# Two-operand elementwise work to VectorE, one-operand copies to GpSimd: batch 0 and the w_out conversion of an attention and feed-forward kernel

## The chip, the cores and the metric

The kernel runs on one core of one Trainium2 chip. The metric is device time in microseconds (us) of one execution, lower is better. Three executions of the kernel before took 678.16, 678.62 and 679.0 us; the median, 678.62, is the figure to which the change is compared.

## The reference

Per head (4 batches, 8 heads, 576 tokens, 64 wide), causal softmax attention is mixed with a linear-attention memory by a gate; the result, seen as 2304 tokens of 512, goes through a feed-forward block with squared ReLU.

```python
scores = scale * q @ k.T                       # causal mask, softmax -> a
local  = a @ v
q_p    = where(q > 0, q, exp(q) - 1) + 1
mem    = (q_p @ M_prev) / (q_p @ z_prev + 1e-6)
x      = g * mem + (1 - g) * local             # g = sigmoid(beta), per head
h = x @ w_in                                   # 512 -> 2048
out = (s * relu(h)**2 + b) @ w_out             # 2048 -> 512
```

## The kernel before

Most large matmuls are done in a fast fp32 format as three products: an operand is split into a high part H (a copy that rounds) and a low part L (the operand minus H), and H*H, H*L and L*H are added in PSUM. So each operand costs one copy and one two-operand subtraction on an elementwise engine, and which of VectorE (DVE), ScalarE (ACT) and GpSimd (POOL) does these is what the change is about.

The first phase walks over 16 pairs of heads. The four pairs of batch 0 (`g < NP`, where `NP` is 4) use plain fp32 operands: `s_red` (line 311) reduces scores from PSUM on DVE and writes them to `P`, `s_exp` (L319) exponentiates on ACT, `s_norm` sums (L326, L327 on DVE) and scales `P` (L331; engine chosen by `dve("nm", ...)`), `pt_bank` transposes `P` on TensorE (L370) and ACT copies it back (L353), `av_mm32` multiplies, and `av_evac` copies the result from PSUM (L432). `x_split` splits that into H (L448) and L (L449). `phi_a` to `phi_c` prepare the memory's queries, `split_qk` (L229) splits scores' operands. Beside all this `w_in` is converted: sixteen `split_w` read 64-bit words with `conv64` (L81 to L84), then make H (L467) and L (L468). `mm1` (L479 to L481, the first feed-forward product) of batch 0 is woven between the heads of batch 1 and so on; its ReLU (`mm1_out`, L488) is on ACT and goes to DRAM.

When attention is done, only `mm1` of the last batch is left on TensorE (PE). Under it `w_out` is converted in eight steps: `conv_u` twice (L81 to L84 on tile `stg`), `t_u` (L654 to L657, sums for a Strassen-like product with seven block products), `split_u` (copies L660 and L664, subtractions L665). `late_b` (L671, L673) makes the H and L of two more blocks; its low part writes into the place of `w1H`, so it waits for the end of `mm1`. The second phase (`t` from 0 to 8) makes for each of seven block products `m` and two halves `c` an operand: `operand` forms a sum or difference for some `m` (L714, L716, L718), its H (L719) and L (L720); `product` (L728 to L730) multiplies, `combine` adds up and stores.

Times at which the helpers are called are a hand-written table of positions (`T`, `at(...)`); the framework then orders each engine's instructions by a timing model of its own. An engine executes its list in order, so an instruction that waits holds up all that stand behind it.

```python
def dve(nm, n, i=None):
    t = T[nm][len(JOBS[n][1])]
    return nc.vector if (t if i is None else t[i]) else nc.gpsimd
```

By `T`, in all pairs of five tiles the third tile's scaling L331 (320 columns) is on DVE and the other four on POOL; the second of the two subtractions of `split_qk` is on DVE and the first on POOL; `x_split`'s subtraction is on POOL.

Of the kernel before, what the change touches and what calls it, by code (L numbers as in the profile page):

```python
# [8 lines left out]
F32 = mybir.dt.float32  # L9
# [3 lines left out]
ALU = mybir.AluOpType  # L13
# [17 lines left out]
def attention_moe_kernel(  # L31
# [15 lines left out]
    nc = tc.nc  # L47
# [87 lines left out]
    def dve(nm, n, i=None):  # L135

        t = T[nm][len(JOBS[n][1])]
        return nc.vector if (t if i is None else t[i]) else nc.gpsimd
# [62 lines left out]
    def phi_b(g):  # L201
        p, r, z = st["q", g], st["r", g], st["z", g]
        nc.vector.scalar_tensor_tensor(p, p, 1.0, r, ALU.min, ALU.add)
        nc.gpsimd.tensor_mul(r, p, z.unsqueeze(1).to_broadcast([128, 5, 2, D]))

    def phi_c(g):
        p, r = st["q", g], st["r", g]
        hp = 2 * parts(g)[1]
        n = ap2.tile([128, 5, 2, 1], F32, tag="nrm", name="nrm")
        nc.vector.tensor_reduce(n, r, AX.X, ALU.add)  # L210
        nc.vector.scalar_tensor_tensor(
            n, n, 1e-6, gin[:, hp:hp + 2].unsqueeze(1).unsqueeze(3).to_broadcast([128, 5, 2, 1]), ALU.add, ALU.mult)
        nc.vector.reciprocal(n, n)
        nc.gpsimd.tensor_mul(p, p, n.to_broadcast([128, 5, 2, D]))

# [208 lines left out]
    def av_evac(x, hi, ps):  # L424
# [6 lines left out]
        if x < 2 * NP:  # L431
            nc.vector.tensor_copy(xo[ma, :], ps[0:64, :n])  # L432
            return
# [24 lines left out]
    def split_w(n):  # L458
# [7 lines left out]
        else:  # L466
            nc.gpsimd.tensor_scalar(H, w, 1.0, 1.0, ALU.mult, ALU.mult)  # L467
        (nc.vector if T["wd"][n] else nc.gpsimd).tensor_sub(L, w, H.bitcast(F32))  # L468

# [180 lines left out]
    def t_u(i, w, s):  # L650
# [5 lines left out]
        nc.vector.tensor_sub(t2, b22, t1)  # L656
        nc.gpsimd.tensor_sub(late32[:, i, 0], t2, b21)  # L657

    def split_u(i, w, s):
        pin(nc.scalar.copy(late32[:, i, 1], w[:, 2]))  # L660
        bHs[i] = w2.tile([128, 5, NE], F32R, tag=f"row{i}", name="bH")
        for x, a, n in ((w[:, 0:1], 0, 1), (w[:, 3:4], 1, 1), (s[:, 0:3], 2, 3)):
            L, H = bLs[:, i, a:a + n], bHs[i][:, a:a + n]
            pin(nc.scalar.copy(H, x))  # L664
            nc.vector.tensor_sub(L, x, H.bitcast(F32))  # L665
# [35 lines left out]
    def operand(t, m, c):  # L701
# [9 lines left out]
        if m in (7, 3):  # L711
            y = x
            x = SUM[c]
            nc.gpsimd.tensor_sub(x, y, A[{7: 21, 3: 11}[m]])  # L714
        elif m == 5:
            nc.vector.tensor_add(x, x, A[22])  # L716
        elif m == 6:
            nc.vector.tensor_sub(x, A[21], x)  # L718
        nc.scalar.copy(H, x)  # L719
        (nc.gpsimd if m in ONPOOL else nc.vector).tensor_sub(L, x, H.bitcast(F32))  # L720

# [143 lines left out]
```

## Time and profile before

| | |
|---|---|
| runs, us | 678.16, 678.62, 679.0 (median 678.62) |
| the profiled execution: its time, its span | 676.45, 674.7 |
| mean granted TensorE clock | 0.98 of full speed |
| busy share of the span: PE, DVE, ACT, POOL | 94%, 72%, 69%, 61% |
| first phase with batch 0 | up to about 122 us |
| w_out conversion on DVE begins | 423.81 us |
| last mm1 matmul ends, first product begins | 477.15 us, 476.99 us |

The span is from the first to the last instruction of the profiled execution; its own time is 1.75 us longer and 2.17 us under the median of the runs. A row for a group of instructions gives their count, their busy time in us, the mean of one in ns, and the idle time of their engine just before them with what ended most of it. Busy time of PE includes time in which matmuls run at a lowered clock.

### The profile page before, as it was taken

Reading aid. Unit: us, or ns where it says so; the run is one execution under the profiler, and the core shown is the slowest. Engines: PE = TensorE matmul, PEld = TensorE weight load, DVE = VectorE, ACT = ScalarE, POOL = GpSimd, SP = SyncE. Lnnn points to the kernel's source line nnn. Section 1 sums busy time; section 2 is a strip of 40 time slices with the busy share of each in tenths; the row PEclk is TensorE's granted clock in tenths of the full one; section 3 lists DMA queues with packets and bytes.
Section 4 is the critical chain, followed back from the end, with each engine's and each line's share of the span. In section 5 each row is a group of like instructions: output and inputs, shape, how many; then the busy total and the mean of one; then the engine's idle time right before and its main releaser. Section 6 shows DMA issues by size and latency. Waiting matters only on the chain. (4 is left out here: it accounts for less than half of the span.)

```text
span 674.7 us, 13026 instructions
## 1 busy us (share of the span) xinstructions
PE 634.6 (94%) x4536; PEld 576.8 (85%) x4536; DVE 487.2 (72%) x1090; ACT 464.0 (69%) x1037; POOL 409.3 (61%) x405
## 2 busy tenths in 40 slices
PE   5989898999999999999999999997699999999998
PEld 2545565889998999999998999997699999999998
DVE  4888879878667757766866641798968887568674
ACT  5566675767667767766866753579888878586841
POOL 3799988776555556555645351341387776666583
PEclk9998899999999999999999999997889999999999
DMA  7987778496677678688875623796643543435301
GB/s 267 232 238 177 197 187 215 161 234 166 166 207 202 165 218 214 162 224 193 198 211 133 162 77 97 286 298 206 206 110 118 165 138 98 116 105 157 94 24 40
DMA packets 73442, 115.75 MB, mean 172 GB/s; under 512 B 10016, under 2 KB 51232, under 8 KB 73376
## 3 DMA queue, kind: packets, MB, share of 16 engines
q1 hardware_dynamic: 73376, 114.91, 61.1%
q8 instruction: 36, 0.59, 0.4%
q14 instruction: 30, 0.25, 0.1%
HBM read 57.68 MB, written 23.59 MB: 120 GB/s over the span
## 5 line engine op out<-in xcount | busy, mean ns | idle before, releaser
L319 ACT ACTIVATE P<-P,mn 128x64 f32<-128x64 f32 (+4 forms) x160 | 89.4, 560 | 48.3 <-DVE mn L311 47.6
L730 PE MATMUL yps<-bH,op 128*128 128x256 f32 x360 | 102.7, 287 | 5.5 <-DVE op L720 5.5
L331 POOL TENSOR_SCALAR P<-P,sm,omg 128x64 f32<-128x64 f32 (+3 forms) x128 | 86.0, 684 | 33.4 <-ACT xc L436 13.5
L728 PE MATMUL yps<-bH,op 128*128 128x256 f32 x360 | 102.7, 286 | 1.3 <-ACT op L719 1.3
L729 PE MATMUL yps<-bL,op 128*128 128x256 f32 x360 | 102.8, 285 | 0.0
L311 DVE CUSTOM_DVE_ANT_0 P<-sps,mask 128x64 f32<-128x64 f32 (+4 forms) x160 | 65.6, 423 | 29.9 <-PE sps L298 23.3
L479 PE MATMUL hps<-xs,w1H 128*128 128x320 f32 (+1 forms) x256 | 79.4, 310 | 5.0 <-ACT r L488 4.8
L479 PE MATMUL hps<-xs,w0H 128*128 128x320 f32 (+1 forms) x256 | 78.8, 310 | 1.6 <-ACT r L488 0.8
L370 PE MATMUL tps<-ident,P 128*128 128x128 f32 (+2 forms) x480 | 76.1, 277 | 2.2 <-POOL P L331 1.3
L481 PE MATMUL hps<-xs,w1L 128*128 128x320 f32 (+1 forms) x256 | 76.9, 300 | 0.0
L480 PE MATMUL hps<-xs,w1H 128*128 128x320 f32 (+1 forms) x256 | 76.8, 300 | 0.0
L480 PE MATMUL hps<-xs,w0H 128*128 128x320 f32 (+1 forms) x256 | 76.2, 299 | 0.0
L481 PE MATMUL hps<-xs,w0L 128*128 128x320 f32 (+1 forms) x256 | 76.1, 298 | 0.0
L730 PEld LDWEIGHTS yps<-bH,op 128*128 128x128 f32 x360 | 69.1, 193 | 6.5 <-DVE op L720 6.4
L728 PEld LDWEIGHTS yps<-bH,op 128*128 128x128 f32 x360 | 69.2, 193 | 1.6 <-ACT op L719 1.6
L729 PEld LDWEIGHTS yps<-bL,op 128*128 128x128 f32 x360 | 69.6, 193 | 0.0
L297 PE MATMUL sps<-X 128*128 128x192 f32 (+1 forms) x180 | 59.9, 337 | 6.1 <-DVE mn L311 3.8
L370 PEld LDWEIGHTS tps<-ident,P 128*128 128x128 f32 (+2 forms) x480 | 55.6, 132 | 11.6 <-issue 5.9
L488 ACT ACTIVATE r<-hps 128x320 f32<-128x320 f32 (+1 forms) x128 | 50.1, 408 | 21.4 <-PE hps L481 15.1
L479 PEld LDWEIGHTS hps<-xs,w1H 128*128 128x128 f32 x256 | 49.3, 193 | 6.5 <-ACT r L488 5.5
L298 PE MATMUL sps<-X 128*128 128x192 f32 (+1 forms) x180 | 53.8, 303 | 0.0
L479 PEld LDWEIGHTS hps<-xs,w0H 128*128 128x128 f32 x256 | 48.8, 191 | 3.9 <-ACT r L488 1.8
(131 smaller groups left out, 1944.5 us busy)
## 6 DMA issues: line engine op xcount, KB each, us to landing
X<-sqk SPq DMA_DIRECT2D x60, 432.0 KB, 6.3
r_d<-r SPq DMA_DIRECT2D x32, 320.0 KB, 4.5
qks<-in_qk_t_dram SPq DMA_DIRECT2D x15, 576.0 KB, 6.5
xa<-in_moe_w_in_dram SPq DMA_DIRECT2D x16, 512.0 KB, 6.4
r_d<-r SPq DMA_DIRECT2D x32, 256.0 KB, 4.3
raw<-in_moe_w_out_dram SPq DMA_DIRECT2D x16, 512.0 KB, 6.7
w1L<-r_d SPq DMA_DIRECT2D x16, 512.0 KB, 4.7
Q<-sqp SPq DMA_DIRECT2D x48, 144.0 KB, 4.1
```

What stands on the lines that cost most here:

```text
L297: nc.tensor.matmul(ps[:, :m], lhsT=lhsT, rhs=X[:, 1, c0:c0 + m], start=True, stop=False)
L298: nc.tensor.matmul(ps[:, :m], lhsT=lhsT, rhs=X[:, 2, c0:c0 + m], start=False, stop=True)
L311: nc.vector.tensor_tensor_reduce(P[:, PO[i] + c0:PO[i] + c0 + n], ps[:, :n], mask[:, mo:mo + n], -SCALE, init, ALU.add, ALU.min, mn[:, o:o ...
L319: nc.scalar.activation(pt, pt, AF.Exp, scale=-1.0, bias=mn[:, o:o + 1], accum_out=sm[:, i:i + 1])
L331: dve("nm", x // 2, i).tensor_scalar(pt, pt, sm[:, i:i + 1], omg[:, h:h + 1], ALU.mult, ALU.mult)
L370: nc.tensor.transpose(ps[0:kn, o:o + qn], P[0:qn, c:c + kn], ident[0:qn, 0:qn])
L479: nc.tensor.matmul(ps, lhsT=wH[:, p, fs], rhs=xs[:, 0], start=p == 0, stop=False)
L480: nc.tensor.matmul(ps, lhsT=wH[:, p, fs], rhs=xs[:, 1], start=False, stop=False)
L481: nc.tensor.matmul(ps, lhsT=wL[:, p, fs], rhs=xs[:, 0], start=False, stop=p == NP - 1)
L728: nc.tensor.matmul(ps, lhsT=H, rhs=BH, start=f == 0, stop=False)
L729: nc.tensor.matmul(ps, lhsT=H, rhs=BL, start=False, stop=False)
L730: nc.tensor.matmul(ps, lhsT=L, rhs=BH, start=False, stop=f == KF - 1)
```

## The change

Within batch 0 (`n < NP` or `g < NP`) every subtraction and product of two tiles goes to VectorE and all five scalings L331 to GpSimd; the copy L432 from PSUM goes to ScalarE. The subtraction L468 of all sixteen `split_w` goes to VectorE. In the w_out conversion L657 goes from GpSimd to VectorE and the copies L660 and L664 from ScalarE to GpSimd. For the first 256 tokens of the second phase (`t == 0`) the H copies go from ScalarE to GpSimd and the differences L714 and the low parts L720 of `m` in 1, 2, 4 from GpSimd to VectorE. The numbers of DMAs, of matmuls and of all other instructions stay, and so do the bytes. In the changed file a line has a number greater by 2 (from L137 of before), and from L713 by 2 to 5.

```diff
--- before.py
+++ after.py
@@ -134,6 +134,8 @@
 
     def dve(nm, n, i=None):
 
+        if n < NP:
+            return nc.gpsimd if nm == "nm" else nc.vector
         t = T[nm][len(JOBS[n][1])]
         return nc.vector if (t if i is None else t[i]) else nc.gpsimd
 
@@ -201,7 +203,7 @@
     def phi_b(g):
         p, r, z = st["q", g], st["r", g], st["z", g]
         nc.vector.scalar_tensor_tensor(p, p, 1.0, r, ALU.min, ALU.add)
-        nc.gpsimd.tensor_mul(r, p, z.unsqueeze(1).to_broadcast([128, 5, 2, D]))
+        (nc.vector if g < NP else nc.gpsimd).tensor_mul(r, p, z.unsqueeze(1).to_broadcast([128, 5, 2, D]))
 
     def phi_c(g):
         p, r = st["q", g], st["r", g]
@@ -211,7 +213,7 @@
         nc.vector.scalar_tensor_tensor(
             n, n, 1e-6, gin[:, hp:hp + 2].unsqueeze(1).unsqueeze(3).to_broadcast([128, 5, 2, 1]), ALU.add, ALU.mult)
         nc.vector.reciprocal(n, n)
-        nc.gpsimd.tensor_mul(p, p, n.to_broadcast([128, 5, 2, D]))
+        (nc.vector if g < NP else nc.gpsimd).tensor_mul(p, p, n.to_broadcast([128, 5, 2, D]))
 
 
     def evac(H_out, L_out, ps, key):
@@ -429,7 +431,7 @@
         xo = st["x", g, hi]
         ma = slice(64 * j, 64 * j + 64)
         if x < 2 * NP:
-            nc.vector.tensor_copy(xo[ma, :], ps[0:64, :n])
+            nc.scalar.copy(xo[ma, :], ps[0:64, :n])
             return
         xc = ap1.tile([128, 320], F32, tag="xc", name="xc")
         co = slice(64 - 64 * j, 128 - 64 * j)
@@ -465,7 +467,7 @@
             nc.scalar.copy(H, w)
         else:
             nc.gpsimd.tensor_scalar(H, w, 1.0, 1.0, ALU.mult, ALU.mult)
-        (nc.vector if T["wd"][n] else nc.gpsimd).tensor_sub(L, w, H.bitcast(F32))
+        nc.vector.tensor_sub(L, w, H.bitcast(F32))
 
 
     def mm1(b, c, f, half):
@@ -654,14 +656,14 @@
         nc.vector.tensor_sub(t1, b12, w[:, 0])
         nc.vector.tensor_sub(t3, b22, b12)
         nc.vector.tensor_sub(t2, b22, t1)
-        nc.gpsimd.tensor_sub(late32[:, i, 0], t2, b21)
+        nc.vector.tensor_sub(late32[:, i, 0], t2, b21)
 
     def split_u(i, w, s):
-        pin(nc.scalar.copy(late32[:, i, 1], w[:, 2]))
+        pin(nc.gpsimd.tensor_scalar(late32[:, i, 1], w[:, 2], 1.0, 1.0, ALU.mult, ALU.mult))
         bHs[i] = w2.tile([128, 5, NE], F32R, tag=f"row{i}", name="bH")
         for x, a, n in ((w[:, 0:1], 0, 1), (w[:, 3:4], 1, 1), (s[:, 0:3], 2, 3)):
             L, H = bLs[:, i, a:a + n], bHs[i][:, a:a + n]
-            pin(nc.scalar.copy(H, x))
+            pin(nc.gpsimd.tensor_scalar(H, x, 1.0, 1.0, ALU.mult, ALU.mult))
             nc.vector.tensor_sub(L, x, H.bitcast(F32))
 
     def late_b(n, part):
@@ -711,13 +713,16 @@
         if m in (7, 3):
             y = x
             x = SUM[c]
-            nc.gpsimd.tensor_sub(x, y, A[{7: 21, 3: 11}[m]])
+            (nc.vector if t == 0 else nc.gpsimd).tensor_sub(x, y, A[{7: 21, 3: 11}[m]])
         elif m == 5:
             nc.vector.tensor_add(x, x, A[22])
         elif m == 6:
             nc.vector.tensor_sub(x, A[21], x)
-        nc.scalar.copy(H, x)
-        (nc.gpsimd if m in ONPOOL else nc.vector).tensor_sub(L, x, H.bitcast(F32))
+        if t == 0:
+            nc.gpsimd.tensor_scalar(H, x, 1.0, 1.0, ALU.mult, ALU.mult)
+        else:
+            nc.scalar.copy(H, x)
+        (nc.gpsimd if m in ONPOOL and t else nc.vector).tensor_sub(L, x, H.bitcast(F32))
 
     def product(t, m):
         ps = ps_y.tile([128, NE], F32, tag="y", name="yps")
```

The framework's order of every engine's list follows from the changed instructions too. Three places of it are shown.

VectorE in batch 0, around the copies of one pair's result (before; `x_561` and `x_568` are the two halves of the result of the second pair, L331 the scaling of `P`):

```order
L331 TENSOR_SCALAR P<-P,sm,omg 128x320
L311 ISA P,mn<-sps,mask 128x320
L311 ISA mn 128x1
L432 COPY x_561<-ops 64x256
...
L82 TENSOR_SCALAR w<-w 128x512
L311 ISA P,mn<-sps,mask,mn 128x288
L311 ISA mn 128x1
L83 SCALAR_TENSOR_TENSOR w<-xa,w 128x512
L84 SCALAR_TENSOR_TENSOR w<-xa,w 128x512
L203 SCALAR_TENSOR_TENSOR qs<-qs,phr 128x640
L432 COPY x_568<-ops 64x320
```

The same place in the changed kernel:

```order
L83 SCALAR_TENSOR_TENSOR w<-xa,w 128x512
L470 TENSOR_TENSOR w0L<-w,w0H 128x512
L451 TENSOR_TENSOR xs<-x_561,xs 128x256
L84 SCALAR_TENSOR_TENSOR w<-xa,w 128x512
...
L329 RECIPROCAL sm<-sm 128x5
...
L313 ISA P,mn<-sps,mask 128x192
L313 ISA mn 128x1
L470 TENSOR_TENSOR w0L<-w,w0H 128x512
L82 TENSOR_SCALAR w<-w 128x512
L451 TENSOR_TENSOR xs<-x_568,xs 128x320
```

The copies and the scaling have left VectorE's list; the low parts of `w_in` (L470, L468 of before) and of the result (L451, L449 of before) stand in it instead, and wait for GpSimd's copies.

GpSimd under the last `mm1`, at the start of the w_out conversion, before:

```order
L449 TENSOR_TENSOR xs<-x_5204,xs 128x320
L657 TENSOR_TENSOR late_5399<-stg 128x256 x4
L714 TENSOR_TENSOR sum_5400<-w0L 128x512
L657 TENSOR_TENSOR late_5399<-stg 128x256 x3
L720 TENSOR_TENSOR op<-w0L,op 128x512 x2
```

and in the changed kernel:

```order
L451 TENSOR_TENSOR xs<-x_5204,xs 128x320
L662 TENSOR_SCALAR late_5399<-stg 128x256
L666 TENSOR_SCALAR bH<-stg 128x256 x2
L666 TENSOR_SCALAR bH<-stg 128x768
L662 TENSOR_SCALAR late_5399<-stg 128x256
```

GpSimd's list is four copies per step there (L662 and L666 are L660 and L664 of before), and one subtraction less.

VectorE where `mm1` ends: L673 waits for its last matmul. Before:

```order
L84 SCALAR_TENSOR_TENSOR stg<-raw,stg 128x512
L673 TENSOR_TENSOR w1H<-late_5399,w0H 128x1024
L673 TENSOR_TENSOR w1H<-late_5399,w0H 128x1024 x2
L655 TENSOR_TENSOR stg<-stg 128x256
L656 TENSOR_TENSOR stg<-stg 128x256
L718 TENSOR_TENSOR w0L<-w0L 128x4x128
L720 TENSOR_TENSOR op<-sum_5400,op 128x512
L665 TENSOR_TENSOR bL<-stg,bH 128x256 x2
L665 TENSOR_TENSOR bL<-stg,bH 128x768
```

and in the changed kernel (L675 is L673 of before, L667 L665, L725 the low part L720):

```order
L725 TENSOR_TENSOR op<-w0L,op 128x512
L675 TENSOR_TENSOR w1H<-late_5399,w0H 128x1024
L675 TENSOR_TENSOR w1H<-late_5399,w0H 128x1024 x2
L667 TENSOR_TENSOR bL<-stg,bH 128x768
L83 SCALAR_TENSOR_TENSOR stg<-raw,stg 128x512
L725 TENSOR_TENSOR op<-w0L,op 128x512
L84 SCALAR_TENSOR_TENSOR stg<-raw,stg 128x512
L725 TENSOR_TENSOR op<-sum_5400,op 128x512
L720 TENSOR_TENSOR w0L<-w0L 128x4x128
L84 SCALAR_TENSOR_TENSOR stg<-raw,stg 128x512
```

More of the conversion (one L83, two L84, one wide L665) now stands behind L673, and the two low parts of the first product (L725 from `w0L`), which were GpSimd's, stand around it.

## Rows read from the trace of the kernel before

**Rows 1.** The page's first part: busy time, share and instructions of each engine.

```profile
PE 634.6 (94%) x4536; PEld 576.8 (85%) x4536; DVE 487.2 (72%) x1090; ACT 464.0 (69%) x1037; POOL 409.3 (61%) x405
```

**Rows 2.** Stretches: length; busy us of PE, PEld, DVE, ACT, POOL; PEclk; DMA.

```profile
20.00:122.00 102.00, 91.64 (x441) 57.01 (x442) 85.96 (x214) 65.28 (x169) 91.86 (x98) 0.95 0.83 211
122.00:400.00 278.00, 273.57 (x2033) 259.50 (x2032) 194.47 (x563) 197.41 (x536) 157.86 (x188) 1.00 0.70 182
423.00:476.00 53.00, 47.68 (x339) 46.77 (x338) 47.05 (x92) 41.90 (x84) 17.42 (x9) 0.94 0.73 256
476.00:500.00 24.00, 17.79 (x116) 16.98 (x115) 19.26 (x23) 21.59 (x36) 12.96 (x10) 0.79 0.56 167
500.00:660.00 160.00, 157.66 (x1313) 156.24 (x1313) 118.86 (x149) 119.61 (x173) 112.08 (x79) 1.00 0.38 112
```

**Rows 3.** PE's waits from 20 to 122 us: us in total, times, longest.

```profile
PE sps L297 <- DVE mn L311: 2.8, 5, 1.0
PE ops L402 <- DVE x L432: 2.7, 4, 1.1
PE sps L297 <- DVE sm L327: 2.0, 1, 2.0
```

**Rows 4.** VectorE's groups by line from 20 to 122 us.

```profile
L83 DVE SCALAR_TENSOR_TENSOR w<-xa,w 128x512 uint32<-128x512 uint32 x12 | 12.7, 1061 | 0.1
L84 DVE SCALAR_TENSOR_TENSOR w<-xa,w 128x512 uint32<-128x512 uint32 x12 | 10.0, 830 | 0.1
L432 DVE COPY x<-ops 64x256 f32<-64x256 f32 (+1 forms) x16 | 7.2, 448 | 4.1 <-PE ops L405 4.0
L82 DVE TENSOR_SCALAR w<-w 128x512 uint32<-128x512 uint32 x12 | 7.0, 584 | 1.2 <-ACT w L81 1.2
L326 DVE TENSOR_SCALAR sm<-sm 128x5 f32<-128x5 f32 x9 | 6.3, 698 | 1.1 <-ACT P L319 1.1
L331 DVE TENSOR_SCALAR P<-P,sm,omg 128x320 f32<-128x320 f32 x10 | 5.9, 591 | 0.1
...
L327 DVE RECIPROCAL sm<-sm 128x5 f32<-128x5 f32 x9 | 1.6, 183 | 0.1
```

**Rows 5.** VectorE's groups by line from 423 to 476 us.

```profile
L83 DVE SCALAR_TENSOR_TENSOR stg<-raw,stg 128x512 uint32<-128x512 uint32 x16 | 10.9, 685 | 0.1
...
L82 DVE TENSOR_SCALAR stg<-stg 128x512 uint32<-128x512 uint32 x16 | 6.9, 433 | 10.3 <-ACT stg L81 10.3
...
L656 DVE TENSOR_TENSOR stg<-stg 128x256 f32<-128x256 f32 x7 | 2.9, 417 | 0.0
```

**Rows 6.** PE in order of time: start, us, instruction, idle before it and releaser.

```profile
459.73 0.63 PE L479 MATMUL hps<-xs,w1H 128*128 128x320 f32 x1 [4.40 <-ACT r L488]
...
484.01 0.39 PE L730 MATMUL yps<-bH,op 128*128 128x256 f32 x1 [4.03 <-DVE op L720]
```

**Rows 7.** GpSimd's groups by line from 20 to 122 us.

```profile
L468 POOL TENSOR_TENSOR w0L<-w,w0H 128x512 fp32r<-128x512 f32 x8 | 10.9, 1367 | 0.0
L204 POOL TENSOR_TENSOR phr<-qs,z 128x640 f32<-128x640 f32 x5 | 9.7, 1945 | 1.4 <-DVE qs L203 1.4
L449 POOL TENSOR_TENSOR xs<-x,xs 128x256 fp32r<-128x256 f32 (+1 forms) x8 | 7.8, 980 | 0.0
L214 POOL TENSOR_TENSOR qs<-qs,nrm 128x640 f32<-128x640 f32 x5 | 7.6, 1521 | 0.9 <-PE sps L298 0.9
...
L468 POOL TENSOR_TENSOR w1L<-w,w1H 128x512 fp32r<-128x512 f32 x4 | 5.1, 1274 | 0.1
...
L467 POOL TENSOR_SCALAR w0H<-w 128x512 fp32r<-128x512 f32 x7 | 5.0, 709 | 3.8 <-DVE nrm L211 2.5 <-DVE w L84 1.3
```

**Rows 8.** ScalarE's groups by line from 423 to 476 us.

```profile
L664 ACT CAST bH<-stg 128x256 fp32r<-128x256 f32 (+1 forms) x21 | 10.8, 555 | 2.3 <-DVE stg L656 2.3
```

**Rows 9.** VectorE in order of time, at the end of mm1.

```profile
477.06 4.49 DVE L673 TENSOR_TENSOR w1H<-late,w0H 128x1024 fp32r<-128x1024 f32 x3 [1.51 <-PE hps L480]
```

**Rows 10.** Waits from 420 to 500 us: us in total, times, longest.

```profile
DVE stg L82 <- ACT stg L81: 10.3, 6, 5.8
```

## The prediction

> **What bounds the kernel now.** First the engines' totals: PE is busy for 634.6 us, far ahead of the others [rows 1], so time can be won only where PE stands still or runs at a lowered clock. The stretches say where [rows 2]. From 122 to 400 us PE is busy for 273.6 of 278 us, from 500 to 660 for 157.7 of 160, both at full clock: what the other engines do there costs next to nothing. Two stages are different. In batch 0 (20 to 122 us) PE has 10.4 us of gaps and a mean clock of 0.95, worth 5.1 us more. From 423 to 500 us, under the w_out conversion and at the handover to the second phase, it has 5.3 + 6.2 us of gaps, at clocks of 0.94 and 0.79. The change acts on just these two stages.
>
> The waits name what ends last. In batch 0 the busiest engine is POOL, 91.9 of 102 us [rows 2], yet PE's long waits are for DVE: 2.8 us for minima, 2.7 for copies of results, 2.0 for sums [rows 3]. DVE is busy for 86.0 us, and part of that is not work: L83 takes 1061 ns there [rows 4] and 685 under the w_out conversion, where POOL has little to do [rows 2, 5]; L326, on five columns, takes 698 where its neighbour L327 on the same tile takes 183 [rows 4]. So POOL's load reaches PE by way of DVE's durations. In the second stage PE stands still for 4.40 us because ACT comes late with the ReLU that frees PSUM, and for 4.03 us because DVE comes late with a low part of the second product [rows 6].
>
> **Batch 0, part by part.** *Removed from DVE*: 16 copies L432, 7.2 us, and 8 of the 10 scalings L331 (those of batch 0), 8 x 0.591 = 4.7 us [rows 4]; together 11.9. *Added to DVE*: in this window 12 low parts L468, 8 low parts L449, L204 and L214 for three of the five pairs seen there, and 3 subtractions L229. None of these runs on DVE before in this shape, so I price them by columns from the nearest two-operand row, L83 at 685 ns for 512 columns [rows 5]: 12 x 0.685 + 8 x 0.385 + 6 x 0.856 + 3 x 0.771 = 8.2 + 3.1 + 5.1 + 2.3 = 18.7 us. That is the low end; if all met POOL as L83 does now, it would be 1061/685 as much, 29.0 us. Net +6.8 at the low end, +17.1 at the high.
>
> *Relief.* On the groups of rows 4 alone the time above the free price is 12 x (1061 - 685) + 12 x (830 - 685) + 12 x (584 - 433) + 9 x (698 - 183) ns = 4.5 + 1.7 + 1.8 + 4.6 = 12.6 us [rows 4, 5]. POOL loses 16.0 us of L468, 7.8 of L449 and three fifths of 17.3 of L204 and L214, 34 of the 41 us of two-operand work in rows 7, and gains 8 scalings, some 4.7 us; it falls from 92 to some 62 us. I take away half of the 12.6, 6.3 us: less than POOL's two-operand time falls, since its copies and scalings stay and DVE has 29 more instructions that can meet them. Bounds: 0 and 12.6.
>
> *Waits.* DVE's 4.0 us of waiting in front of L432 [rows 4] goes: ACT waits there instead, which has 36.7 us free in the stretch [rows 2] and behind which stand exponentials and transposed copies. What is new is that DVE waits for POOL's H copies (20 times). The order gives each some DVE instructions of distance, and a copy takes 0.709 us [rows 7]; I put 1 us in all, between 0 and 20 x 0.36 = 7. ScalarE gains 16 copies of about 0.45 us, hidden in those 36.7 us; were they not, they would hold up the exponentials by up to 7 us.
>
> Sum for the stage: +6.8 - 6.3 - 4.0 + 1.0 = **-2.5 us** of DVE's time. I let PE follow DVE one for one, because PE's three waits above are all for DVE.
>
> **The handover.** ACT loses the copies: 10.8 us of L664 by 476 us [rows 8], and L660 and the fourteen H copies of `t == 0` besides. The 4.40 us gap before 459.73 should go, as ACT's list then holds little but ReLUs, L81 and the squaring. But that gap hides: DVE reaches L673 at 475.6 and waits only 1.51 us for the end of mm1 [rows 9], so an earlier end of mm1 gives DVE at most those 1.5 us. Beyond that DVE sets the pace. Ahead of L673 it gains seven L657 at 0.417 (priced as L656, the same shape) [rows 5], one L714 and one L720 at 0.685, 4.3 us; a wide L665, an L83 and two L84, some 3.0 us, move behind. Of its 10.3 us of waiting for L81 the longest, 5.8, lies ahead of the conversion [rows 10]; of the other 4.5 us I take half, 2.2, as saved by the freed ACT. POOL's copies beside it cost DVE some 1 us. So L673 starts 1.5 - 1.3 + 2.2 - 1.0 = 1.4 us earlier. From there to the low part that ended the 4.03 us gap it was 4.49 us of L673 and on to 484.01, 6.9 us in all [rows 6, 9]; now it is three L673, the wide L665, L83, L720, L84, L720, about 7.3. That part comes 1.0 us earlier; the low parts of the eighth step of w_out, which the first product needs, come some 3 us behind it, against PE's 2 us of work, so the small later stalls stay. **-1 us**, between -8 (both gaps and their lowered clock gone) and +6 (PE waits for the whole of DVE's extra 4.3 us, and longer at half clock).
>
> No DMA is added, dropped or resized; w_out's rows are loaded into places that the H copies free, now in POOL's list, which is all but empty there (17.4 of 53 us [rows 2]). SP's queue passes the same transfers.
>
> **The sum.** 676.45 - 2.5 - 1.0 = 672.95 for the profiled execution, which lies 2.17 us under the median of the runs; so I expect **675.1 us** against 678.62.
>
> **The rivals.** *A, slower: DVE becomes the engine that never catches up in batch 0.* It is the only one of the three whose free-price work grows, from 86 us busy of 102. If the 18.7 us cost the middle between free and contended, 23.8, relief is only 4 us, and the waits for POOL's copies are 4 us, then 23.8 - 11.9 - 4 - 4 + 4 = +8, and with the handover 685.6 us. It decides as soon as relief and DVE's saved wait are under 7.9 us together. For it: POOL still has 62 us of work, and it holds up mostly the instructions that DVE now has more of. Against: L83 at 685 ns beside a lightly loaded POOL. The Trainium skill (SBUF — State Buffer, Who interferes with whom) states that a DVE instruction with two SBUF inputs contends with any GpSimd instruction that reads SBUF, and that the later one is blocked to the other's end; by that rule one-operand copies block as well, which is this rival's case, and no row above separates them from the two-operand ones.
>
> *B, no change.* The two stages are set by DVE's total, relief equals the added work less the saved waits, and the 4.40 us gap is given back at L673: 678.6 us. For it: mm1's end was waited for by DVE for just 1.51 us.
>
> *C, much faster.* PE's gaps go: 10 of the 15.5 us in batch 0 (gaps and clock) need only that DVE be in time, and the two gaps in rows 6 take half a clock of several us with them; half of each stage's loss is 8 + 8 us, to 662.6. Against: DVE has more to do, not less.
>
> **How the numbers follow.** My forecast (a gain of 1.4 to 9 us) has 0.42, C 0.13, B 0.15, A 0.24, and a handover that gets worse by more than batch 0 gains 0.06. A measurement of this kernel can tell 0.2%, 1.36 us, from no change. So faster 0.55, same 0.15, slower 0.30. The range runs from 666, half way to C, to 685, just short of A's full price; 2 in 10 lie outside.
>
> **What would show it.** In the changed profile: L83 in batch 0 under 900 ns and L326 under 450; POOL near 62 us from 20 to 122 us; no L432 among PE's waits; no 4 us gap of PE for L488, but still one of 3 to 7 us for a low part after mm1. It is wrong if DVE in batch 0 is busy over 95% with PE waiting for it longer than now (A), or if new rows of DVE waiting for POOL's copies add up to more than 3 us; and wrong the other way if PE's gaps in batch 0 halve.

## The result and the profile after

The changed kernel took **684.36 us** (median of 10 runs, 679.85 to 689.92), the kernel before 678.81 us (10 runs, 676.74 to 682.99): a ratio of 1.0077 with a 95% interval of 1.0048 to 1.0106. It is slower by 0.8%, where 0.5% faster was forecast. The profiled execution took 682.7 us, with a span of 680.9 us. Executions more than 1.5% above the fastest of their kernel are left out of all ratios but not out of the medians, and the profile of e13 below is of such an execution.

Line numbers of the changed kernel are 2 higher than before's from L137 on, and 5 higher from L725 on; the first tokens' H copy is L722, the H copy of all others L724. The page's first part (as [rows 1]):

```profile
PE 636.2 (93%) x4536; PEld 578.2 (85%) x4536; DVE 500.1 (73%) x1119; ACT 450.7 (66%) x1007; POOL 384.7 (57%) x406
```

The stretches, with the columns of [rows 2]:

```profile
20.00:122.00 102.00, 93.33 (x464) 60.21 (x464) 87.25 (x223) 70.47 (x182) 69.45 (x80) 0.95 0.80 208
122.00:400.00 278.00, 273.19 (x2052) 260.86 (x2051) 194.85 (x564) 199.26 (x540) 156.49 (x186) 1.00 0.69 183
423.00:476.00 53.00, 43.32 (x319) 42.15 (x319) 49.32 (x88) 28.00 (x51) 24.24 (x31) 0.95 0.71 234
476.00:500.00 24.00, 19.57 (x107) 18.03 (x105) 22.12 (x32) 10.29 (x11) 13.22 (x14) 0.68 0.36 111
500.00:660.00 160.00, 152.97 (x1255) 150.00 (x1255) 115.29 (x147) 117.55 (x169) 107.34 (x77) 1.00 0.37 112
```

Batch 0 came out as intended: GpSimd falls from 91.9 to 69.5 us, VectorE carries more instructions in nearly the same time, PE is busier by 1.7 us. Two lines are bad. From 476 to 500 us PE's mean clock is 0.68 (0.79 before, when `mm1` ended 9.3 us later, so the stretch held other work), and from 500 to 660 us, which the prediction took as settled, PE is busy for 152.97 us against 157.66.

VectorE's groups from 20 to 122 us (as [rows 4]):

```profile
L83 DVE SCALAR_TENSOR_TENSOR w<-xa,w 128x512 uint32<-128x512 uint32 x13 | 10.3, 793 | 0.1
L84 DVE SCALAR_TENSOR_TENSOR w<-xa,w 128x512 uint32<-128x512 uint32 x13 | 9.8, 751 | 0.0
L82 DVE TENSOR_SCALAR w<-w 128x512 uint32<-128x512 uint32 x13 | 9.4, 724 | 0.6 <-ACT w L81 0.6
...
L470 DVE TENSOR_TENSOR w0L<-w,w0H 128x512 fp32r<-128x512 f32 x8 | 6.1, 768 | 3.1 <-POOL w0H L469 3.1
L451 DVE TENSOR_TENSOR xs<-x,xs 128x256 fp32r<-128x256 f32 (+1 forms) x8 | 4.9, 610 | 0.0
...
L328 DVE TENSOR_SCALAR sm<-sm 128x5 f32<-128x5 f32 x9 | 2.7, 295 | 0.8 <-ACT P L321 0.7
```

PE's waits in the same stretch (as [rows 3]):

```profile
PE tps L372 <- POOL P L333: 2.8, 3, 1.4
PE ops L404 <- ACT x L434: 2.8, 2, 1.5
PE sps L299 <- DVE mn L313: 2.2, 3, 0.9
```

The conversion's L83 fell from 1061 to 793 ns, the five-column L328 from 698 to 295; L82 rose from 584 to 724. Two of PE's three waits changed their owner, from VectorE to GpSimd's scalings and ScalarE's result copies, and PE still gained. The first mm1 matmul behind the attention (the start of mm1's last quarter; **T** below) came at 411.9 us where it was 416.8: **4.9 us won**, of which 2.0 had been won by the first mm1 matmul of batch 0 (115.0 us for 117.0), about the end of batch 0's part.

One pair of traces measures this roughly. Up to 20 us before T all engines' lists are the same in the change and in all of e1 to e18 below but e8, which has those of before. In seventeen of these eighteen traces (without e13) T lies between 409.9 and 418.9 us, 414.6 on average; in the two with the lists of before it is 416.8 and 418.9.

PE at the handover, in order of time (as [rows 6]), the matmuls behind waits of 0.99 us and more:

```profile
453.26 0.39 PE L481 MATMUL hps<-xs,w1H 128*128 128x256 f32 x1 [1.00 <-ACT r L490]
457.68 0.39 PE L481 MATMUL hps<-xs,w1H 128*128 128x256 f32 x1 [1.29 <-ACT r L490]
464.75 0.39 PE L481 MATMUL hps<-xs,w1H 128*128 128x256 f32 x1 [1.05 <-ACT r L490]
471.08 0.58 PE L733 MATMUL yps<-bH,op 128*128 128x256 f32 x1 [3.20 <-POOL op L722]
475.02 0.58 PE L735 MATMUL yps<-bH,op 128*128 128x256 f32 x1 [3.14 <-DVE op L725]
480.50 0.58 PE L735 MATMUL yps<-bH,op 128*128 128x256 f32 x1 [2.12 <-DVE op L725]
...
488.44 0.58 PE L733 MATMUL yps<-bH,op 128*128 128x256 f32 x1 [0.99 <-POOL op L722]
```

The 4.40 us gap for the ReLU is three gaps of about 1 us, and mm1 ends 9.3 us earlier than before. Then the first product waits 3.20 us for an H copy on GpSimd, and two low parts follow with 3.14 and 2.12 us. GpSimd in order of time says why that H copy is late:

```profile
461.61 0.52 POOL L662 TENSOR_SCALAR late<-stg 128x256 f32<-128x256 f32 x1 [7.37 <-DVE stg L84]
462.10 0.77 POOL L666 TENSOR_SCALAR bH<-stg 128x256 fp32r<-128x256 f32 x2
465.32 1.21 POOL L666 TENSOR_SCALAR bH<-stg 128x768 fp32r<-128x768 f32 x1 [2.45 <-DVE stg L658]
468.16 1.05 POOL L662 TENSOR_SCALAR late<-stg 128x256 f32<-128x256 f32 x1 [1.63 <-DVE stg L84]
469.18 1.10 POOL L666 TENSOR_SCALAR bH<-stg 128x256 fp32r<-128x256 f32 x2
470.25 0.78 POOL L722 TENSOR_SCALAR op<-w0L 128x512 fp32r<-128x512 f32 x1
```

The copy at 470.25 stands in GpSimd's list behind the sixth and seventh step of w_out, whose copies wait 7.37, 2.45 and 1.63 us for VectorE. VectorE's groups from 423 to 476 us (as [rows 5]):

```profile
L667 DVE TENSOR_TENSOR bL<-stg,bH 128x256 fp32r<-128x256 f32 (+1 forms) x20 | 13.5, 685 | 1.3 <-POOL bH L666 1.3
L84 DVE SCALAR_TENSOR_TENSOR stg<-raw,stg 128x512 uint32<-128x512 uint32 x12 | 9.3, 786 | 0.0
L83 DVE SCALAR_TENSOR_TENSOR stg<-raw,stg 128x512 uint32<-128x512 uint32 x12 | 8.6, 734 | 0.0
L82 DVE TENSOR_SCALAR stg<-stg 128x512 uint32<-128x512 uint32 x13 | 6.5, 497 | 2.3 <-ACT stg L81 2.3
```

L83 and L82 were 685 and 433 ns; 12 to 13 tiles are converted by 476 us where 16 were. The last of w_out's eight steps ends 82.3 us behind T (69.8 before).

In the steady phase ScalarE, GpSimd and PE show one chain, in order of time:

```profile
605.22 1.07 ACT L698 ACTIVATE w1L<-w1L 128x1024 f32<-128x1024 f32 x1 [2.37 <-DMA w1L<-r_d]
606.19 0.60 ACT L724 CAST op<-w1L 128x512 fp32r<-128x512 f32 x1
...
608.80 1.12 ACT L724 CAST op<-w1L 128x512 fp32r<-128x512 f32 x2
```

```profile
609.48 3.79 POOL L725 TENSOR_TENSOR op<-w1L,op 128x512 fp32r<-128x512 f32 x3 [1.19 <-ACT op L724]
```

```profile
610.81 0.39 PE L735 MATMUL yps<-w0H,op 128*128 128x256 f32 x1 [0.76 <-POOL op L725]
```

A square of the next block's tokens waits 2.37 us for its load at the head of ScalarE's list; behind it stand the present block's last H copies, behind those GpSimd's low parts, and PE waits for these. PE's waits from 500 to 660 us (as [rows 3]), before:

```profile
PE yps L730 <- POOL op L720: 1.7, 4, 0.7
PE yps L730 <- DVE op L720: 0.6, 2, 0.3
```

and in the changed kernel:

```profile
PE yps L735 <- DVE op L725: 3.4, 6, 1.6
PE yps L735 <- POOL op L725: 3.4, 5, 0.9
```

So the trace splits at two points: T, and **B1**, the first matmul of the second block of tokens. Up to T the change wins 4.9 us; from T to B1 it loses 7.1 (97.7 us for 90.6); from B1 to the last matmul it loses 4.1 (168.2 for 164.1).

### The profile page after: what moved, and what is told of

Its sections match the earlier page's. It is cut to its first block, busy times and chain, and to the rows that moved or that the text cites. A ratio compares the mean times of both kernels' runs of the same rounds, so it can differ in the third digit from the quotient of the medians.

```text
span 680.9 us, 13014 instructions
## 1 busy us (share of the span) xinstructions
PE 636.2 (93%) x4536; PEld 578.2 (85%) x4536; DVE 500.1 (73%) x1119; ACT 450.7 (66%) x1007; POOL 384.7 (57%) x406
## 5 line engine op out<-in xcount | busy, mean ns | idle before, releaser
L333 POOL TENSOR_SCALAR P<-P,sm,omg 128x64 f32<-128x64 f32 (+4 forms) x136 | 97.9, 731 | 61.6 <-DVE sm L329 45.2
L735 PE MATMUL yps<-bH,op 128*128 128x256 f32 x360 | 104.4, 292 | 8.2 <-DVE op L725 8.2
L733 PE MATMUL yps<-bH,op 128*128 128x256 f32 x360 | 104.5, 291 | 5.5 <-POOL op L722 5.2
L481 PE MATMUL hps<-xs,w1H 128*128 128x320 f32 (+1 forms) x256 | 78.4, 306 | 3.5 <-ACT r L490 3.3
L735 PEld LDWEIGHTS yps<-bH,op 128*128 128x128 f32 x360 | 70.3, 196 | 10.4 <-DVE op L725 10.3
L481 PE MATMUL hps<-xs,w0H 128*128 128x320 f32 (+1 forms) x256 | 77.7, 306 | 0.8 <-DVE pt L224 0.4
L733 PEld LDWEIGHTS yps<-bH,op 128*128 128x128 f32 x360 | 70.8, 197 | 6.6 <-POOL op L722 6.0
L482 PE MATMUL hps<-xs,w1H 128*128 128x320 f32 (+1 forms) x256 | 76.0, 297 | 0.0
L482 PE MATMUL hps<-xs,w0H 128*128 128x320 f32 (+1 forms) x256 | 75.6, 296 | 0.0
L299 PE MATMUL sps<-X 128*128 128x192 f32 (+1 forms) x180 | 60.2, 337 | 2.5 <-DVE mn L313 2.2
```

Source lines behind the costliest of these rows:

```text
L299: nc.tensor.matmul(ps[:, :m], lhsT=lhsT, rhs=X[:, 1, c0:c0 + m], start=True, stop=False)
L333: dve("nm", x // 2, i).tensor_scalar(pt, pt, sm[:, i:i + 1], omg[:, h:h + 1], ALU.mult, ALU.mult)
L481: nc.tensor.matmul(ps, lhsT=wH[:, p, fs], rhs=xs[:, 0], start=p == 0, stop=False)
L482: nc.tensor.matmul(ps, lhsT=wH[:, p, fs], rhs=xs[:, 1], start=False, stop=False)
L733: nc.tensor.matmul(ps, lhsT=H, rhs=BH, start=f == 0, stop=False)
L735: nc.tensor.matmul(ps, lhsT=L, rhs=BH, start=False, stop=f == KF - 1)
```

## The experiments

Three parts can be had one by one: **A** (batch 0 and w_in: `dve`, `phi_b`, `phi_c`, `av_evac`, `split_w`), **B** (w_out: `t_u`, `split_u`) and **C** (the first block's operands). Each kernel was timed beside the kernel before, whose median was between 678.3 and 679.5 us each time; by the intervals, a difference of two kernels is uncertain by some 3 to 5 us. The two right columns are from each one's profile, a single execution. e2 and e14, and e3 and e15, have the same lists from T to B1 but for the last instructions, and differ there by 1.7 and 2.6 us, so smaller differences of that column are not read.

| kernel | us | ratio to before, interval | T to B1 | B1 to end |
|---|---|---|---|---|
| before | 678.8 | | 90.6 | 164.1 |
| the change (A+B+C) | 684.36 | 1.0077 (1.0048 to 1.0106) | 97.7 | 168.2 |
| e1 A | 678.07 | 0.9981 (0.9948 to 1.0014) | 88.0 | 171.0 |
| e2 A+C | 680.63 | 1.0038 (1.0002 to 1.0074) | 90.8 | 171.4 |
| e3 A+B+C, first H copies on ACT | 677.22 | 0.9973 (0.9934 to 1.0012) | 94.3 | 164.0 |
| e4 A+B | 686.24 | 1.0108 (1.0047 to 1.0169) | 96.2 | 168.3 |
| e5 A, ACT's list of before | 673.98 | 0.9929 (0.9895 to 0.9963) | 88.0 | 168.3 |
| e6 A, late squares | 668.58 | 0.9837 (0.9796 to 0.9878) | 88.5 | 160.3 |
| e7 A+B+C, ACT's list of before | 686.77 | 1.0098 (1.0062 to 1.0134) | 97.4 | 169.3 |
| e8 before, late squares | 675.30 | 0.9928 (0.9896 to 0.9960) | 89.8 | 159.8 |
| e9 A+B+C, late squares | 675.51 | 0.9932 (0.9901 to 0.9962) | 98.2 | 159.8 |
| e10 e9, ACT's order at the conversion | 676.82 | 0.9946 (0.9914 to 0.9978) | 94.9 | 159.8 |
| e11 e6 + w_out's subtractions | 669.43 | 0.9834 (0.9796 to 0.9872) | 88.2 | 159.7 |
| e12 e6 + w_out's copies | 673.97 | 0.9911 (0.9873 to 0.9948) | 97.1 | 159.8 |
| e13 e6 + idle copies | 672.86 | 0.9901 (0.9865 to 0.9937) | not read | 160.3 |
| e14 e6 + C | 666.30 | 0.9807 (0.9759 to 0.9855) | 89.1 | 159.7 |
| e15 e9, first H copies on ACT | 670.22 | 0.9870 (0.9825 to 0.9915) | 91.7 | 159.7 |
| **e16** e15, w_out's copies on ACT | **664.85** | **0.9770 (0.9720 to 0.9819)** | 86.8 | 159.7 |
| e17 e16 + idle copies | 670.95 | 0.9898 (0.9841 to 0.9955) | 89.6 | 159.7 |
| e18 e16, first H copies on GpSimd | 671.31 | 0.9862 (0.9805 to 0.9919) | 89.9 | 159.8 |

### Which part loses: e1 to e4

**e1**: only A's edits of the diff.

> Only the part on batch 0 and on w_in's conversion is made; w_out's conversion and the first tokens' operands stand as before. The theories differ on what lost some 7 us between the last matmul of mm1 and the second product and 4 us more near 555 to 635 us. Theory Q (GpSimd's queue: the first operands' H copies stand behind w_out's copies, which wait for VectorE), theory D (22 more two-operand instructions on VectorE in the handover) and theory L (w_out's conversion itself comes late, whatever the operands do) all expect the gain of batch 0 to arrive whole: 4.9 us less than before, 673.9 us (672.5 to 675.5). Theory S (the steady phase loses as soon as the schedule before it is shifted at all, whichever part shifts it) expects 677 to 679 us: the gain at the start of mm1's last part, and about 4 us lost after 550 us.

678.07 us, as S has it and no other theory: TensorE won 2.6 us by B1 beyond what T gave, and lost 6.9 after it.

**e2**: A and C.

> Batch 0's part and the first tokens' operands (H copies to GpSimd, subtractions to VectorE) are made, w_out's conversion stands as before. Q: no w_out copies stand on GpSimd, only its eight subtractions, so the H copies come in time: 673 to 675 us. D: 12 to 14 of the 22 added VectorE instructions are left, so about half of the handover's loss: 677 to 679 us. L: like Q, 673 to 675 us. S: 677 to 679 us with the loss after 550 us.

680.63 us: S again, with some 2 us more.

**e3**: A, B and C, with this line as before:

```
-            nc.gpsimd.tensor_scalar(H, x, 1.0, 1.0, ALU.mult, ALU.mult)
+            nc.scalar.copy(H, x)
```

> Everything of the change but one piece: the first tokens' H copies stay on ScalarE. Q: the handover's loss is gone and the 4.4 us that mm1's last part gained beside batch 0's 4.9 are kept: 669.5 to 673 us, and the first product starts within 1 us of mm1's end. D: VectorE carries all 22 instructions as in the changed kernel: 681 to 684 us. L: w_out's conversion is as late as in the changed kernel: 680 to 684 us. S: 674 to 677 us, the handover's loss gone and the later one kept.

677.22 us, 7 below the change: D and L fall as the main cause, since all the instructions added to VectorE are in (18 by the diff, not the 22 that the expectations say: eight for w_out, four differences and six low parts). But by the traces only 3.4 us of it lie between T and B1 and 4.2 after B1, and the first product starts 1.7 us after mm1's end, where Q had it within 1. So Q is at most half of it.

**e4**: A and B.

> Batch 0's part and w_out's conversion are made, the first tokens' operands stand as before (H copies on ScalarE, the low parts of the first operand and two differences on GpSimd). Q: on GpSimd the low parts of the first operand now stand behind all of w_out's copies but four, and wait as the H copies did: 680 to 685 us. D: only 8 of the 22 added instructions are left: 674 to 677 us. L: 680 to 684 us, with the same lateness of w_out's tiles as in the changed kernel. S adds 4 us after 550 us to any of these.

686.24 us, the slowest of these four: B costs in the handover, with or without C. Q foresaw it; so did L.

### The steady phase: e5 to e8

**e5** and **e7** record ScalarE's instructions from the third block on and tie each to the one before it in the order that the kernel before has (O H copy, S square, A scaling, U copy of a product):

```
+    ORDER = "OOSOOSOAOOAOOSOSOAOAOUOOSOSOAOAO..."
+    line = [AQ[k].pop() for k in reversed(ORDER)]
+    for b, a in zip(line, line[1:]):
+        tc.add_manual_dep(b.ins, a.ins.name, ...)
```

> The part on batch 0 and w_in alone (as in e1_batch0), and ScalarE's list from the third block of tokens on is set to the kernel before's, instruction kind by instruction kind (H copies, squares, scalings, U copies). In e1_batch0 the stretch from the second block's first product to the end took 171 us, before 164. Theory S' (the loss in the steady phase is ScalarE's list: with the squares of the next block one or two places further ahead, they wait for their transfer in front of the H copies of the present block): 164 to 166 us for that stretch, 670 to 673 us in all. Theory M (an early start of the blocks is only eaten by waits for the loads, in whatever order ScalarE works): 170 to 172 us for the stretch, 677 to 679 us in all.

> The whole change, and ScalarE's list from the third block on is the kernel before's. In the changed kernel the stretch from the second block to the end took 168 us, before 164. S': 164 to 165 us for the stretch, 680 to 681 us in all, what is left above before being the handover's. M: 168 us and 684 us as in the changed kernel.

673.98 us, 4.1 under e1, and 686.77, 2.4 above the change. After B1, 168.3 us in e5 (171.0 without the tie) and 169.3 in e7 (168.2). With the same list as before the stretch did not take before's 164.1: the list alone is not the cause, and S' in that form falls.

**e6** (on A) and **e8** (on the kernel before) keep the squares behind all that ScalarE was given ahead of them:

```
-        nc.scalar.activation(r, r, AF.Square)
+        (pin if t > 1 else same)(nc.scalar.activation(r, r, AF.Square))
```

> The part on batch 0 and w_in alone, and from the third block on each square is kept behind all H copies that the program gives to ScalarE ahead of it, so that it no longer stands in front of the present block's last H copies. S': no square waits for its transfer in front of an H copy, TensorE's waits for low parts go: 161 to 164 us from the second block to the end, 667 to 671 us in all. M: 677 to 679 us. Should the squares now come too late for the next block's first operands, TensorE waits for those instead, and the time is 680 us or more.

> The kernel before, with the squares kept behind the H copies as in e6_batch0_latesq. S': the waits of 0.2 to 0.7 us that TensorE has from 583 us on go, and the slower blocks with them: 161 to 163 us from the second block to the end, 675 to 677 us in all. M: no change, 678 to 679 us. With squares too late: 681 us or more.

668.58 and 675.30 us; the stretch after B1 takes 160.3 and 159.8 us, and PE has not one wait of 0.15 us in it. One line of the windows of e6, 500 to 655 us:

```profile
500.00:655.00 155.00, 154.97 (x1303) 154.54 (x1302) 108.64 (x148) 118.69 (x170) 114.16 (x79) 1.00 0.38 114
```

M falls. What costs is not which of these lists ScalarE has, but that in all of them a square can stand at the head and meet its load late: with the squares held back the loss is gone, in the kernel before too. A start 5 to 7 us earlier (e1, e2) was eaten whole, but when a square meets its load late is not shown: e4 and e7, whose second block starts 5 to 8 us later than before's, lose 4 to 5 us as well. From here on all kernels have the late squares, so that only T to B1 differs.

### Inside w_out's part: e9 to e12

**e9** is the change with e6's line.

> The whole change, with the later squares of e6_batch0_latesq, so that the steady phase no longer differs: what is left between this and e6_batch0_latesq (668.6 us) is the price of w_out's conversion and the first operands as the change has them. From the traces (97.5 us from the first matmul of mm1's last quarter to the second block, 88.3 with batch 0's part alone) about 9 us: 676 to 679 us. If the loss in the handover hung on the steady phase's order, 669 to 672 us.

675.51 us: 6.9 above e6, and 98.2 us from T to B1 against 88.5.

**e10**: e9, and ScalarE's absolute values (b), first squares (S), scalings (A) and late copies (l) tied in before's order.

```
+    line = [next(at0[k]) for k in "SASlbAbSSbbAAlbb"]
```

> As e9_all_latesq, and on ScalarE the absolute values of w_out's last six tiles, the first block's squares and scalings and the copies of the late products' high parts follow one another in the kernel before's order. Theory T-list (freed of w_out's copies, ScalarE takes the first block's squares and scalings ahead of w_out's sixth step, whose absolute values start 3.8 us later, and steps 6 to 8 of the conversion end 5, 9 and 12 us later): most of the loss goes, 669 to 673 us, and step 8 of the conversion ends within 74 us of the start of mm1's last quarter (82 in the changed kernel, 70 before). Theory T-copy (GpSimd's 32 copies, which wait for VectorE's sums and make VectorE's subtractions wait, are what makes each step long): 675 to 679 us, step 8 ends at 78 us or later. Theory T-dve (VectorE's added subtractions): 675 to 679 us too.

676.82 us, step 8 ends 79.2 us behind T (82.7 in e9): T-list falls. By the trace the order gives back 3.3 us between T and B1, by the medians nothing.

**e11** and **e12** split B, on e6: `t_u`'s subtraction to VectorE alone, and `split_u`'s two copies to GpSimd alone.

> e6_batch0_latesq with one piece more of the change: the eight subtractions for the late products' parts of w_out go from GpSimd to VectorE (0.41 us each there). T-dve: 671 to 674 us. T-list and T-copy: 667 to 670 us, perhaps a little less than e6_batch0_latesq, since ScalarE waited 5 us for these subtractions.

> e6_batch0_latesq with the other piece: w_out's 32 H copies go from ScalarE to GpSimd, the eight subtractions and the first operands stay as before. T-copy: 674 to 678 us, from the copies alone. T-list: 674 to 678 us too, since ScalarE is as free as in the whole change; a run between 667 and 671 us would say that the copies do no harm without the rest.

669.43 and 673.97 us. The subtractions cost nothing (T-dve falls; ScalarE no longer waits for them on GpSimd), the copies 5.4 us, 8.6 by the traces (e12's is of the longest of its eight executions). VectorE's groups in e12, 415 to 490 us:

```profile
L665 DVE TENSOR_TENSOR bL<-stg,bH 128x256 fp32r<-128x256 f32 (+1 forms) x21 | 17.2, 822 | 4.8 <-POOL bH L664 4.8
L84 DVE SCALAR_TENSOR_TENSOR stg<-raw,stg 128x512 uint32<-128x512 uint32 x16 | 12.7, 796 | 0.0
L83 DVE SCALAR_TENSOR_TENSOR stg<-raw,stg 128x512 uint32<-128x512 uint32 x16 | 12.1, 771 | 0.1
L82 DVE TENSOR_SCALAR stg<-stg 128x512 uint32<-128x512 uint32 x16 | 8.5, 538 | 6.1 <-ACT stg L81 6.0
```

Both costs are in it: these instructions took 662, 683, 685 and 421 ns in e6, and VectorE waits 4.8 us for the copies, for which it waited in e6 not at all.

### Sharing or waiting, and the first H copies: e13 to e18

**e13**: e6, with as many columns copied by GpSimd from the identity tile onto itself in the first six of the eight steps.

```
             pin(nc.scalar.copy(H, x))
+            for _ in range(2 * n if i < 6 else 0):
+                pin(nc.gpsimd.tensor_scalar(ident, ident, 1.0, 1.0, ALU.mult, ALU.mult))
```

> e6_batch0_latesq (668.6 us), ScalarE's 32 copies of w_out where they were, and beside them, for the first six of the eight steps, as many columns copied by GpSimd from the identity tile onto itself, behind the same step's subtraction; nobody waits for these copies. Theory T-share (VectorE and GpSimd slow each other when both read and write SBUF): VectorE's conversion instructions grow from 0.60 us to 0.66 us or more on average as in e12_copies_pool (0.70), and the time goes to 671 to 674 us. Theory T-chain (the copies cost because each step waits for them): 668 to 670 us, VectorE's instructions as in e6_batch0_latesq.

672.86 us, in T-share's range. But in its trace the idle copies stood ahead of `t_u`'s subtractions on GpSimd, for which ScalarE waited 15.2 us in place of 5.0, so the run does not separate the two. e17 comes nearer to it.

**e14** is e6 with C; **e15** is e9 with the first H copies on ScalarE (e3's line).

> e6_batch0_latesq plus the first tokens' operands as the change has them, w_out's conversion as before. If the first operands' H copies on GpSimd only cost where they stand behind w_out's copies: 667 to 670 us. If they cost by themselves (1.3 us on GpSimd for 0.6 on ScalarE): 671 to 673 us, as e2_batch0_first against e1_batch0 would have it (2.6 us).

> e9_all_latesq (675.5 us) with the first tokens' H copies left on ScalarE: the price of standing behind w_out's copies. If e3_firstH_on_act's 7 us under the changed kernel are mostly that: 670 to 672 us. If most of them were the steady phase: 673 to 675 us.

666.30 and 670.22 us. C as a whole, its subtractions included, costs nothing here (2.3 us under e6, though e2 was 2.6 above e1). With w_out's copies on GpSimd, the first H copies there cost 5.3 us (e9 against e15; 6.5 by these traces, 3.4 by those of the change and e3). That they cost it by standing behind w_out's copies is not shown, for with the H copies on ScalarE the first product waits as long, now for ScalarE (e15):

```profile
471.94 0.36 PE L728 MATMUL yps<-bH,op 128*128 128x256 f32 x1 [3.38 <-ACT op L719]
```

**e16**: A, `t_u`'s subtraction and the first operands' subtractions on VectorE, no copy moved.

> The change without any copy moved to GpSimd, with the later squares: batch 0's part, the late products' subtractions and the first tokens' subtractions on VectorE, all H copies of w_out and of the operands on ScalarE. T-dve would have 672 to 675 us. Without it 666 to 669 us, at or a little under e6_batch0_latesq, since the first operand's low parts no longer wait on GpSimd.

**664.85 us**, 2.3% under before: the best kernel of this study. Against e15 it differs by w_out's 32 copies alone: 5.4 us once more (4.9 by the traces).

**e17**: e16 with idle copies from the H tiles onto the identity tile.

```
             pin(nc.scalar.copy(H, x))
+            for a in range(2 * n + (n == 1)):
+                nc.gpsimd.tensor_scalar(ident, H[:, a // 2 % n, :128].bitcast(F32), 1.0, 1.0, ALU.mult, ALU.mult)
```

> e16_subs_dve (664.9 us) with idle copies on GpSimd in all eight steps of w_out's conversion: 96 copies of 128 columns out of the H tiles onto the identity tile, right behind ScalarE's H copies; GpSimd has nothing else to do in that stretch, and nobody waits for these copies. T-share: VectorE's conversion instructions take 0.65 us or more on average (0.60 in e16_subs_dve), and the time is 667 to 670 us. T-chain (the real copies cost because each conversion step waits for them): 664 to 666 us, VectorE's instructions up by less than 0.03 us.

670.95 us. VectorE's groups of e16, 417 to 492 us:

```profile
L665 DVE TENSOR_TENSOR bL<-stg,bH 128x256 fp32r<-128x256 f32 (+1 forms) x24 | 13.9, 596 | 2.4 <-ACT bH L664 2.4
L84 DVE SCALAR_TENSOR_TENSOR stg<-raw,stg 128x512 uint32<-128x512 uint32 x16 | 11.0, 685 | 0.1
L83 DVE SCALAR_TENSOR_TENSOR stg<-raw,stg 128x512 uint32<-128x512 uint32 x16 | 10.8, 686 | 0.1
L82 DVE TENSOR_SCALAR stg<-stg 128x512 uint32<-128x512 uint32 x16 | 6.8, 422 | 8.4 <-ACT stg L81 8.4
```

And of e17, 416 to 491 us, with GpSimd's idle copies under them:

```profile
L667 DVE TENSOR_TENSOR bL<-stg,bH 128x256 fp32r<-128x256 f32 (+1 forms) x24 | 15.3, 654 | 0.0
L84 DVE SCALAR_TENSOR_TENSOR stg<-raw,stg 128x512 uint32<-128x512 uint32 x16 | 11.7, 734 | 0.1
L83 DVE SCALAR_TENSOR_TENSOR stg<-raw,stg 128x512 uint32<-128x512 uint32 x16 | 11.3, 719 | 0.1
L82 DVE TENSOR_SCALAR stg<-stg 128x512 uint32<-128x512 uint32 x16 | 7.4, 460 | 6.9 <-ACT stg L81 6.9
```

```profile
L666 POOL TENSOR_SCALAR ident<-bH 128x128 f32<-128x128 f32 x83 | 57.3, 690 | 15.7 <-ACT bH L664 8.9
```

The time is just above T-share's range, the growth of L82 to L84 (0.598 to 0.638 us on average) just under its bound, and both are over what T-chain allows; VectorE is slowed by 5 to 10% by one-operand copies that no conversion step waits for. From T to B1 the two differ by 2.8 us, by the medians by 6.1. The run's tail is not quite clean: the last idle copies hold up GpSimd's first difference for the second block, for which VectorE waits 3.0 us. How much of the real copies' 5.4 us is sharing and how much the steps' own waits stays open.

**e18**: e16 with C's H copies on GpSimd.

> e16_subs_dve with the first tokens' H copies on GpSimd, as the change has them; w_out's copies stay on ScalarE. If these copies only cost behind w_out's: 663 to 667 us. If they cost by themselves, 1.3 us on GpSimd for 0.6 us on ScalarE in front of the first products: 667 to 669 us.

671.31 us, 6.5 above e16 and over both ranges. Its profiled run was the shortest of the six, 664.49 us; from T to B1 it took 3.1 us more than e16. e14, which differs from e18 by `t_u`'s subtractions alone, was 2.3 us under e6. With nothing ahead of it on GpSimd the first H copy starts 0.9 us before mm1's end (in the change 2.4 us after it), and PE waits only 0.29 us for the first product:

```profile
464.93 1.90 POOL L719 TENSOR_SCALAR op<-w0L 128x512 fp32r<-128x512 f32 x2 [52.40 <-ACT bH L664]
```

So w_out's copies do delay that copy, but the H copies seem to cost about as much without them. What they cost by themselves stays open, between a gain of 2 and a loss of 6 us.

## Why the prediction was wrong

**Batch 0: the direction right, the number in part luck.** -2.5 us was forecast. The trace shows -2.0 at the first mm1 matmul and -4.9 at T, the traces with and without A -3.3 at T on average, and e6 against e8, which differ by A alone, -6.7 by the medians. The marks held: L83 under 900 ns, L328 under 450, no wait of PE for the result copies on VectorE. The relief on the four groups was 3.2 us on L83, 1.0 on L84, 3.6 on the sums and -1.7 on L82, in all 6.1 where 6.3 was put. But the added VectorE work was priced too low: 22.4 us for what costs 18.6 at the free price (L470 took 768 ns for 685, L451 610 for 385), near rival A's 23.8. VectorE's waits for GpSimd's H copies were 3.4 us where 1 was put, over the mark of 3. With these terms (added, taken off, relief, the old wait, the new ones) the prediction's own sum is 22.4 - 12.1 - 6.1 - 4.0 + 3.4 = +3.6 us of VectorE's time, a loss, and PE gained all the same: that PE follows VectorE one for one did not hold. Of PE's waits for VectorE, the 2.0 us for a sum are gone and those for minima fell from 2.8 to 2.2; the wait for L432 did not vanish, 2.8 us of it reappeared on ScalarE. Where the rest of the gain comes from stays open. GpSimd kept 69.5 us, not 62: the scalings on it grew by 11.4 us (28.9 to 40.3) where 4.7 were put. Rival A did not come: VectorE was busy for 87.3 of 102 us.

**The handover: the step that failed.** It was put at -1 us with a worst case of +6, and cost 7.1. The sentence that failed is that GpSimd's list "is all but empty there" and that its copies beside VectorE cost "some 1 us". By busy time it was empty; but its new copies wait for VectorE and hold up what stands behind them, and VectorE waits for them. The L673 that was to start 1.4 us earlier starts 63.0 us behind T (L675) where it was 60.2. Two terms were missed. w_out's copies on GpSimd: 5.4 us (e12 against e6, e15 against e16), partly because they lengthen the instructions of a VectorE that is the bound there (49.3 of 53 us busy). And the first operands' H copies on GpSimd: 5.3 us (e9 against e15), of which neither e15 nor e18 shows that the place behind w_out's copies is the cause, though the trace shows them held up there. The Trainium skill (SBUF — State Buffer, Who interferes with whom), which the prediction gave to rival A in batch 0, says that a VectorE instruction with two SBUF inputs contends with any GpSimd instruction that reads SBUF; e17 bears it out for one-operand copies (L665 from 596 to 654 ns). In batch 0 the added instructions were longer than priced as well, but the place where it is shown to cost time is the conversion. What the prediction had right is the form of the gaps: none of 4 us for the ReLU, and one of 3.14 us for a low part after mm1. The seven subtractions L657, 2.9 of the 4.3 us that the step counted against VectorE, cost nothing (e11).

**The steady phase: the step that was not made.** "What the other engines do there costs next to nothing" was read from 157.7 of 160 us busy. The trace of before had 2.3 us of waits for low parts there, that of the change 6.8; behind them stood squares that meet late loads, worth some 4 us to the kernel before (e8 against before) and 9 to the changed one (e9 against 684.36). The change touches only the first block's operands in that phase, but it moves the phase's start; with ScalarE's order of before tied, the loss stayed (e5, e7).

The pieces, from medians: A -6.7 (e6 against e8); the two groups of subtractions -3.7 (e16 against e6); w_out's copies +5.4 (e15 against e16); the first H copies with them +5.3 (e9 against e15); the steady phase's greater loss some +5 (9 against 4). That they sum to the measured +5.6 is no test, since each piece begins where another ends. Each is uncertain by 3 to 5 us: the gain of A and the two losses from copies are clear of that, the gain from the subtractions is not.

## What to carry to other kernels

An engine with little busy time is not a free place: before moving work there, ask what will stand behind it in that engine's list, what each piece waits for, and whether the work lengthens the instructions of the engine that is the bound beside it. Here two-operand subtractions could move to VectorE for nothing, copies to the idle GpSimd could not. The price of a stage that a change hardly touches can still move with the stage's start: a prefetch whose consumer stands at the head of an in-order list can turn an earlier start into waits, and holding that consumer back by one line was worth 4 us to the kernel before and 9 to the changed one. Test parts of a change on top of a version in which the later stages are clean, or their losses hide in one another.

## What the hardware showed

GpSimd's copies with one operand slow VectorE's instructions beside them, two-operand ones (L83 from 686 to 719 ns, L84 from 685 to 734) as well as the one-operand L82 (422 to 460), when GpSimd is busy for 57.3 of 75 us (e17). I had expected the two-operand form on GpSimd to be the culprit. It lengthens them too: with `t_u`'s eight subtractions on GpSimd (1.90 us each, e6) VectorE's L655 takes 687 ns, with only these moved to VectorE 560 (e11), and with GpSimd's part of the first operands moved as well 418 (e16).

PE's granted clock was at the lower of its two levels (1.2 of 2.4 GHz) from 471.0 to 484.6 and from 488.0 to 494.9 us in the changed kernel, 20.5 us in all. The first of these falls begins at the end of the 3.20 us gap, and the gaps of 3.14 and 2.12 us lie within it. In the kernel before it was from 457.6 to 464.4, within and behind the 4.40 us gap, and from 484.9 to 495.2, behind the 4.03 us gap [rows 6], 17.1 us in all.
